# Attention followed by a maxout feed-forward layer on one core: who issues the loads of phi for batches 2 to 7

## The chip, the cores and the metric

The kernel runs on one core of one Trainium2 chip. The metric is the device time of one execution in microseconds (us), lower is better. Three runs of the kernel before the change give its time; one further execution was taken with the hardware profiler, and all durations below that are not called a median come from that one.

Engines are named as in the profile: PE is TensorE (matmuls), PEld its weight loads, DVE is VectorE, ACT is ScalarE, POOL is GpSimd, SP is SyncE, which here does nothing but issue DMAs. Sixteen DMA engines move all data. L95 is line 95 of the kernel.

## The reference

```python
a   = exp(phi - max) / sum(exp(phi - max))            # over the 576 positions; phi: 8 x 8 x 576 x 32
k_m = einsum('bhsm,bhsd->bhmd', a, k)                  # k, v, q: 8 batches x 8 heads x 576 x 64
v_m = einsum('bhsm,bhsd->bhmd', a, v)
attn = softmax(q @ k_m^T / 8)                          # 32 memory slots a head
x = (attn @ v_m) put back to rows of 512               # 4608 x 512
h = maximum(maximum(x @ w1, x @ w2), x @ w3)           # w1, w2, w3: 512 x 768
out = h @ w_out                                        # w_out: 768 x 512; out: 4608 x 512, float32
```

All inputs and the output are float32 in HBM.

## The kernel before, in words

One batch is one round of work. For batch b the kernel loads phi(b), k(b), v(b) and q(b); takes the exponential of phi (step E, ACT, L260); contracts it with k and v on PE (step B, L280); normalizes (N, DVE); turns the small result (K, or k for batches 2 to 7); transposes q on DVE (Q); makes scores on PE (S, L387) and their exponential on ACT (L396); normalizes over the slots (steps a, s, c, m and X, where m is a multiplication on POOL, L463); folds the small value matrix into the weights (D, PE, L494); and runs the feed-forward layer (F, L520 and L533; T, L567 and L582). Step T ends with a tile of 128 rows of the output in SBUF and a DMA to HBM that SP issues (L607). The first fold (D@0) needs w1; steps W, O and J before it prepare products of w3 and w_out and need those two.

Nothing of the order is left to a scheduler. A long list of tokens such as `L0@2` (step L0 of batch 2) is walked from left to right, and each engine gets its instructions in that order. Every engine's queue is in order: an instruction that waits holds back all that were issued behind it on the same engine. The token `L0@b` is `load_ph(b)`, `L1@b` and `L2@b` load k and v, `L3@b` loads q, `Y0` to `Y3` load w1, w2, w3 and w_out, and `H` loads half of k(0) or v(0).

Who issues which DMA before the change:

- SP issues phi(0), in two halves, at the very start (L93), and all output tiles but the last half one (L607, L636).
- POOL issues everything else that is loaded: k, v (L99), q (L112), phi(1) to phi(7) (L95), w1, w2, w3 (L118) and w_out (L125). k, v, q and the weights are turned from float32 to bf16 on the way; phi stays float32. Each issue takes about 0.75 us of POOL, which also runs the multiplications (L463), the repacking of k and v for batches 2 to 7 (L105) and half of the small moves (L344).

In the profile the DMAs that POOL issues are queue q0 (software_dynamic), those of SP are q1 (hardware_dynamic). The program tells of the landing of a DMA by one of eight semaphores for each of the two queues, in turn, so an issue also waits until the DMA eight places before it on its own queue has landed.

The tile for phi has two buffers (`inp`, bufs=2). phi(b) may only be loaded when the exponential of batch b-2 has read the buffer, so phi(2) waits for E@0, phi(3) for E@1, and so on. A first part of the token list shows where the loads of batch 1 and 2 stand:

```
E@0 H0@0 H2@0 L3@0 Z25@0 B0@0 ... Y2@0 G0@0 ... Y3@0 ... H1@0 H3@0 Y0@0 ... Y1@0 O1@0
L1@1 B1@0 N1@0 L0@1 O2@0! L3@1 K1@0! L2@1 ... V1@0 F0@0 F6@0 L2@2 ... L1@2 p1@0 L0@2 ...
```

`G0` makes POOL wait for the second half of k(0) before it issues more; `Z` are matmuls of zeros that keep PE busy at the start.

Of the kernel before, what the change touches and what calls it, by code (L numbers as in the profile page):

```python
# [15 lines left out]
def kernel(  # L16
# [12 lines left out]
    nc = tc.nc  # L29
# [50 lines left out]
    def by_pair(src, b):  # L80
        return src[b].rearrange("h s d -> (h s) d").rearrange(
            "(j p c) d -> p j (c d)", p=P, c=NC
        )
# [3 lines left out]
    def load_ph(b):  # L87
        ph = inp.tile([P, NP, NC, M], FP32, name="ph")
        loaded.setdefault(b, {})["ph"] = ph
        dst = ph.rearrange("p j c m -> p j (c m)")  # L90
        if b == 0:
            for h in halves:
                nc.sync.dma_start(out=dst[:, h], in_=by_pair(phi, b)[:, h])  # L93
        else:
            nc.gpsimd.dma_start(out=dst, in_=by_pair(phi, b))  # L95

# [32 lines left out]
    def wait_for(b, n):  # L129

        x = loaded[b]["q"][0:1, 0, 0, 0:2] if n else loaded[b]["kv"][0:1, 1, NP - 1, 0, 0:2]
        nc.gpsimd.tensor_copy(out=gate, in_=x)

    load_ph(0)

    warm = const.tile([P, BANK], BF16, name="warm")
# [504 lines left out]
    def issue(b, n, swap):  # L641
# [4 lines left out]
            + [nc.gpsimd.memset(x[:, :, :, 2 * D : 2 * D + 1], 1.0) for x in kvrs],  # L646
            "Y": lambda: load_w(i) if i < 3 else load_wo(),
            "L": lambda: load_ph(b) if i == 0 else load_q(b) if i == 3 else load_kv(b, i - 1),
            "H": lambda: load_kv(b, i % 2, halves[i // 2]),
            "r": lambda: pack(b, i),  # L650
# [28 lines left out]
    for w in """  # L679
# [24 lines left out]
        n, b = w.rstrip("!^").split("@")  # L704
# [31 lines left out]
```

## Time and profile before

| what | value |
|---|---|
| median of 3 runs | 163.14 us (162.96 to 163.16) |
| time of the profiled execution | 162.81 us |
| its span, first to last instruction | 161.0 us |
| granted PE clock | 1.00 throughout |
| PE busy | 152.3 us, 95% of the span |
| DVE, ACT, POOL busy | 113.9, 97.0, 81.9 us |
| phi(1) to phi(7), issued by POOL (L95) | 7 x 0.78 us, first at 13.5, last at 105.9 us |
| issue to landing of all phi loads | 3.0 to 22.5 us, median 13.4 |
| E@0 (ACT, L260) | from 3.73 to 5.15 us |

The profiled execution lies 0.33 us under the median, and 1.8 us of its time lie outside the span. In the views below a wait is put down to whatever ended it last; the chain of waits is read from the last instruction back to the first, and shows only what set the end.

### The profile page before, as it was taken

To read this page: it belongs to the slowest core of one execution; us is meant where nothing else is said; L and a number is where in the kernel's file an instruction comes from. 1 tells how busy PE (TensorE), PEld (TensorE's weight loads), DVE (VectorE), ACT (ScalarE), POOL (GpSimd) and SP (SyncE) were. 2 spreads that over 40 slices of the span, in tenths; PEclk is the share of its full clock that TensorE was granted. 3 is DMA by queue.
4 is the path that set the end of the run, shared out by engine and by line. 5 is a ranking of instruction groups with operands and counts; after the bars stand their busy time and mean duration, and the time that the engine had idled before them with its cause. 6 is when DMAs were issued, how large, how long until landed. Compare 5 with 4: busy or idle time off the path is not lost.

```text
span 161.0 us, 4938 instructions
## 1 busy us (share of the span) xinstructions
PE 152.3 (95%) x2062; PEld 84.9 (53%) x2062; DVE 113.9 (71%) x222; ACT 97.0 (60%) x179; POOL 81.9 (51%) x120
## 2 busy tenths in 40 slices
PE   7977799999999999999999999999999999999990
PEld 2432454664467446754674447656554377744460
DVE  2023456999889866877894998999898969752440
ACT  3205413934686779887997998689579884511000
POOL 7275124100699779389939989666907250000000
PEclk9999999999999999999999999999999999999999
DMA  5999999999999999999999999999712330004433
GB/s 157 147 206 208 207 209 210 242 247 210 228 312 263 275 242 269 256 259 231 269 280 258 207 310 299 218 224 284 174 69 90 116 125 0 0 0 172 158 130 132
DMA packets 21974, 31.77 MB, mean 197 GB/s; under 512 B 1216, under 2 KB 16576, under 8 KB 21952
## 3 DMA queue, kind: packets, MB, share of 16 engines
q0 software_dynamic: 16080, 21.43, 69.6%
q1 hardware_dynamic: 5728, 9.90, 17.6%
q8 instruction: 16, 0.26, 0.6%
q10 hardware_dynamic: 144, 0.13, 0.2%
q14 instruction: 6, 0.05, 0.1%
HBM read 39.32 MB, written 9.44 MB: 303 GB/s over the span
## 4 chain that ended last, share of the span: by engine, by line
PE 77%; DMA 14%; POOL 4%; DVE 2%; issue 1%; ACT 0%; POOLq 0%
PE psum L520 30%; PE psum L582 27%; DMA w_sb<-in_moe_w_dram 9%; PE psum L567 8%; PE psum L494 5%; DMA kvo<-in_k_dram 4%; PE psum L280 3%; PE psum L387 2%; POOL kvo L99 2%; PE psum L558 1%; POOL t L463 1%; DVE qT L367 1%; PE psum L618 1%; POOL wo_sb L125 0%; DVE hT L533 0%
## 5 line engine op out<-in xcount | busy, mean ns | idle before, releaser
L582 PE MATMUL psum<-wo_sb,hT 128*128 128x512 bf16 x210 | 51.3, 380 | 0.0
L520 PE MATMUL psum<-attn,wp 128*128 128x288 bf16 x384 | 50.2, 286 | 0.2 <-DVE attn L471 0.2
L520 PEld LDWEIGHTS <-wp 128*128 128x128 bf16 x384 | 37.1, 98 | 13.3 <-issue 1.3
L533 DVE TENSOR_TENSOR hT<-psum,h 128x576 bf16<-128x576 f32 x48 | 33.8, 746 | 4.9 <-PE psum L520 2.4
L582 PEld LDWEIGHTS <-hT 128*128 128x128 bf16 x210 | 19.1, 98 | 24.0 <-issue 4.8
L190 ACT CAST wp<-psum 128x1024 bf16<-128x1024 f32 (+2 forms) x33 | 26.4, 860 | 6.5 <-PE psum L494 6.5
L188 ACT ACTIVATE h<-psum 128x576 bf16<-128x576 f32 (+1 forms) x41 | 23.0, 598 | 6.4 <-PE psum L520 4.8
L105 POOL COPY kvr<-kvo 128x2304 bf16<-128x2304 bf16 x12 | 25.3, 2111 | 0.8 <-DMA kvo<-in_v_dram 0.4
L344 POOL COPY kvt<-kvm 32x96 bf16<-32x96 bf16 x48 | 12.4, 259 | 13.9 <-DVE kvm L335 6.7
L463 POOL TENSOR_TENSOR t<-t,sm 128x576 bf16<-128x576 bf16 x14 | 16.0, 1155 | 6.3 <-DVE sm L458 6.0
L567 PE MATMUL psum<-wp,attn 128*128 128x512 bf16 x62 | 18.1, 379 | 0.0
L194 DVE COPY ot<-psum 128x512 f32<-128x512 f32 x15 | 10.2, 677 | 9.9 <-PE psum L567 5.8
L190 ACT COPY ot<-psum 128x512 f32<-128x512 f32 x20 | 11.7, 592 | 8.6 <-PE psum L567 6.0
L99 POOL DMA_DIRECT2D kvo<-in_v_dram x9 | 6.6, 739 | 16.5 <-PE psum L280 13.1
L344 ACT COPY kvt<-kvm 32x96 bf16<-32x96 bf16 x48 | 12.9, 269 | 2.0 <-DVE kvm L335 1.2
L168 PE MATMUL psum<-warm 128*128 128x512 bf16 x44 | 11.8, 421 | 1.2 <-DVE warm L137 1.2
L367 DVE STREAM_TRANSPOSE qT<-qq 128x576 f32<-128x576 f32 x16 | 11.7, 749 | 1.3 <-DMA qq<-in_q_dram 1.3
L396 ACT ACTIVATE e<-psum 128x576 bf16<-128x576 f32 x16 | 9.5, 650 | 4.6 <-PE psum L387 4.5
L260 ACT ACTIVATE e<-ph 128x1152 bf16<-128x1152 f32 (+1 forms) x9 | 9.5, 1056 | 4.6 <-DMA ph<-in_phi_dram 4.4
L441 DVE STREAM_TRANSPOSE t<-e 128x288 f32<-128x288 f32 x14 | 6.6, 470 | 5.6 <-ACT e L396 5.5
L449 DVE TENSOR_REDUCE sm<-t 128x18 f32<-128x576 bf16 x14 | 10.3, 739 | 0.2
L192 DVE TENSOR_SCALAR h<-psum 128x288 bf16<-128x288 f32 (+1 forms) x17 | 9.4, 575 | 0.8 <-ACT ot L190 0.4
(62 smaller groups left out, 137.5 us busy)
## 6 DMA issues: line engine op xcount, KB each, us to landing
out_dram<-ot SPq DMA_DIRECT2D x35, 256.0 KB, 5.8
qq<-in_q_dram POOLq DMA_DIRECT2D x8, 576.0 KB, 13.5
kvo<-in_k_dram POOLq DMA_DIRECT2D x7, 576.0 KB, 16.2
ph<-in_phi_dram POOLq DMA_DIRECT2D x7, 576.0 KB, 14.3
kvo<-in_v_dram POOLq DMA_DIRECT2D x7, 576.0 KB, 17.8
w_sb<-in_moe_w_dram POOLq DMA_DIRECT2D x3, 768.0 KB, 15.1
wo_sb<-in_moe_w_out_dram POOLq DMA_DIRECT2D x1, 768.0 KB, 10.8
ph<-in_phi_dram SPq DMA_DIRECT2D x2, 288.0 KB, 3.1
```

The costliest lines, as they stand in the source:

```text
L105: nc.gpsimd.tensor_copy(out=kvrs[b % 2][:, :, :, D * i : D * (i + 1)], in_=kvos[b % 2][:, 1 - i])
L168: nc.tensor.matmul(po[:, 0:BANK], lhsT=warm[:, 0:P], rhs=warm, start=True, stop=True)
L188: nc.scalar.activation(out=out_, in_=in_, func=AF.Relu)
L190: nc.scalar.copy(out=out_, in_=in_)
L344: move(out=kvt[R * x : R * (x + 1), :, r], in_=kvm[r, x])
L367: nc.vector.transpose(out=s["qT"][:, j].rearrange("p j c r e -> p (j c r e)").bitcast(FP32), in_=loaded[b]["q"][:, j].rearrange("p j c d - ...
L449: nc.vector.tensor_reduce(out=sm, in_=s["t", g].rearrange("p n r e -> p n e r"), op=ALU.add, axis=mybir.AxisListType.X,)
L463: nc.gpsimd.tensor_tensor(out=t, in0=t, in1=s["sm", g].unsqueeze(2).to_broadcast([P, S // HP, R, 2]), op=ALU.mult,)
L520: nc.tensor.matmul(acc[:, h, 0:SH], lhsT=wps[b][:, g, w * DF + ft * P : w * DF + (ft + 1) * P], rhs=attn[:, g, c0 : c0 + SH], start=(g == ...
L533: nc.vector.tensor_tensor(out=hT[:, ft, (b % 2) * S : (b % 2 + 1) * S].rearrange("p (h n) -> p h n", h=2), in0=a, in1=s["h1", ft], op=ALU.max,
L567: nc.tensor.matmul(po, lhsT=attn[:, g, c0 : c0 + P], rhs=wp3s[b][:, g, :], start=(g == 0 and not done), stop=(last and g == NG - 1),)
L582: nc.tensor.matmul(po, lhsT=hT[:, fc, c0 : c0 + P], rhs=wo_sb[:, fc, :], start=(n == ns[0] and not done), stop=(last and n == ns[-1]),)
```

## The change

phi(2) to phi(7) are issued by SP instead of POOL, each at the place in the token list where it stood. phi(0) stays on SP in two halves, phi(1) stays on POOL.

```diff
     def load_ph(b):
         ...
         if b == 0:
             for h in halves:
                 nc.sync.dma_start(out=dst[:, h], in_=by_pair(phi, b)[:, h])
+        elif b > 1:
+            nc.sync.dma_start(out=dst, in_=by_pair(phi, b))
         else:
             nc.gpsimd.dma_start(out=dst, in_=by_pair(phi, b))
```

SP's queue after the change, in order: phi(0) in two halves, phi(2), two output tiles, phi(3), two tiles, phi(4), eight tiles, phi(5), three tiles, phi(6), three tiles, phi(7), and the remaining seventeen and a half. POOL's queue is the one before without six of its seven L95. What the two queues' instructions wait for otherwise is the same rule as before: a buffer that is free, and the DMA eight places before on the same queue. All lines behind L93 move down by two; this text uses the numbers of the kernel before.

## The prediction

> **What bounds the kernel now.** I read the page first (its busy times, its DMA row, its queues).
>
> ```profile
> PE 152.3 (95%) x2062; PEld 84.9 (53%) x2062; DVE 113.9 (71%) x222; ACT 97.0 (60%) x179; POOL 81.9 (51%) x120
> ...
> DMA  5999999999999999999999999999712330004433
> ...
> q0 software_dynamic: 16080, 21.43, 69.6%
> q1 hardware_dynamic: 5728, 9.90, 17.6%
> ```
>
> Two resources look full: PE over the whole span, and the DMA engines, whose row shows 9 from the second slice (4 us) to slice 29 (about 117 us). An average can't say which of them sets the end, so the chain of waits is next: start, length, what.
>
> ```profile
> 2.12 6.78 DMA kvo<-in_k_dram
> ...
> 9.13 0.77 POOL wo_sb L125
> ...
> 11.29 15.10 DMA w_sb<-in_moe_w_dram
> 26.39 0.14 issue
> 26.53 1.06 PE psum L494 x40
> ...
> 41.64 0.74 POOL kvo L99
> ...
> 45.25 5.79 PE psum L520 x46
> ```
>
> Until 26.39 us the chain is loads: k(0), and then w1, for which the first fold waits. From 26.53 it is PE almost without a break. The table of windows gives the two halves in numbers (columns: stretch, length, busy us of PE, PEld, DVE, ACT, POOL, clock, DMA share, GB/s written).
>
> ```profile
> 2.00:4.00 2.00, 2.00 (x6) 0.76 (x5) 0.00 (x0) 0.29 (x2) 1.93 (x5) 1.00 0.99 300
> 5.00:6.00 1.00, 1.00 (x7) 0.45 (x5) 0.00 (x0) 0.14 (x1) 0.02 (x1) 1.00 0.81 99
> 6.00:7.00 1.00, 1.00 (x6) 0.43 (x5) 0.00 (x0) 0.00 (x0) 0.00 (x0) 1.00 1.08 149
> 7.00:8.00 1.00, 1.00 (x6) 0.39 (x4) 0.00 (x0) 0.00 (x0) 0.00 (x0) 1.00 1.11 182
> ...
> 12.00:16.00 4.00, 2.93 (x42) 0.98 (x40) 1.36 (x2) 2.04 (x4) 2.33 (x4) 1.00 1.18 208
> 5.20:26.40 21.20, 17.82 (x265) 8.45 (x262) 7.32 (x14) 5.22 (x10) 8.33 (x12) 1.00 1.17 200
> 26.50:157.40 130.90, 130.49 (x1787) 74.89 (x1787) 105.64 (x201) 88.75 (x166) 69.64 (x96) 1.00 0.86 200
> ```
>
> From 26.5 to 157.4 us PE is busy 130.49 of 130.90 us: 0.41 us of idle time is all that any change behind the start can win. From 5.2 to 26.4 us the DMA engines are over 100% (packets overlap) and deliver a steady 200 GB/s of converted data: here the kernel is bound by bytes. So it is "loads until w1 is there, then 131 us of PE". A microsecond put in front of w1 is a microsecond at the end.
>
> **Where phi(2) goes.** The timeline of POOL, and then that of ACT, fix its old and new place.
>
> ```profile
> 12.78 0.79 POOL L99 DMA_DIRECT2D kvo<-in_k_dram  x1
> 13.51 0.81 POOL L95 DMA_DIRECT2D ph<-in_phi_dram  x1
> ...
> 26.94 0.75 POOL L95 DMA_DIRECT2D ph<-in_phi_dram  x1 [1.72 <-issue]
> ```
>
> ```profile
> 3.73 1.42 ACT L260 ACTIVATE e<-ph 128x576 bf16<-128x576 f32 x2 [1.71 <-DMA ph<-in_phi_dram]
> ```
>
> Before, phi(2) is the L95 at 26.94 us, behind w1, w2, k(1), phi(1), q(1), v(1), v(2) and k(2) on POOL's queue; it takes 22.5 us from issue to landing (49.4 us). After the change it is SP's third DMA, and nothing stands in front of it but phi(0). It waits only for its buffer, which E@0 gives back at 3.73 + 1.42 = 5.15 us. So it is issued at about 5.2 us, while q(0), w3 and half of k(0) are still under way and w_out, v(0) and w1 have not even been issued. The token that puts phi(2) "at its place" orders it on SP's queue alone, where the first output tile comes at 39.5 us; it does not hold it behind the loads of another queue.
>
> **Its price.** All loads that flow behind phi(2) land later by as much time of the DMA engines as phi(2) takes. Two rows bound that. On POOL's queue: k(1) and phi(1) are issued one after the other in a queue that is always full, and the view of their lines gives 20.3 and 21.1 us from issue to landing:
>
> ```profile
> DMA to landing us min/median/max: 20.3/20.3/20.3
> ```
>
> ```profile
> DMA to landing us min/median/max: 21.1/21.1/21.1
> ```
>
> k(1) lands at 12.78 + 20.3 = 33.1, phi(1) at 13.51 + 21.1 = 34.6 us, so 576 KB of phi occupy the engines for 1.5 us. On SP's queue: phi(0), the same bytes, flows nearly alone from 2 to 4 us at 300 GB/s; 0.59 MB at that rate are 1.97 us. A full price between them is likely, because the engines are shared: 1.7 us, nearer to the first row, since that is the one with the engines saturated. Below both lies what fits into room that the old queue leaves: from 5 to 8 us it delivers 99, 149 and 182 GB/s against 208 later, 0.19 MB less. If phi(2) filled all of that, a third of it would be free and the price 1.97 x 2/3 = 1.3 us; most of its data should come later, so I don't take this. The Trainium skill ("DMA: Bandwidth & Descriptors", Where 436 GB/s comes from) has a ceiling of 435 GB/s for the fabric; by it 0.59 MB would cost an estimated 1.35 us and the sum would be 164.5 us. The row is preferred, as the converted loads here read 2 x 200 = 400 GB/s at most.
>
> Could anything absorb it? PE waits for w3 at 16.0, w_out at 19.96 and w1 at 26.53 us, each right behind its landing, and then for phi(1) (E@1 starts at 34.62, on its landing) and v(1). All these loads stand behind phi(2) in time, so all shift together, and PE's work between them has no room (14.37 of 14.50 us busy from 26.5 to 41). Only behind 45 us does the missing phi(2) on POOL's queue (it took its turn before 49.4 us) give the DMA engines back what they lent; there PE is the bound and has no use for it.
>
> **The rest of the move.** POOL loses 6 issues x 0.78 = 4.7 us. POOL is on the chain from 41.64 to 44.69 us (v(3)'s issue, two multiplications L463), but phi(3)'s issue at 44.62 stands behind those, and phi(2)'s at 26.94 falls into idle time: worth 0. The cover is PE's own work; without it the gain would be at most the 0.41 us of idle time. phi(3) to phi(7) go from POOL's place to SP's: phi(3) to about 41.6 us for 44.6, phi(4) to about 51 for 52.5 (it waits for E@2, which ends at 50.7 us; the tile behind it is due at 54.6), phi(5) to 75.9 for 73.5, phi(6) to 90.1 for 88.1, phi(7) to 97.0 for 105.9. Each lands sooner than now, as SP's transfers took 6 us in the loaded stretch and POOL's 14. The loads they pass on the shared engines lose 1.5 to 2 us each time, but have gained the same from phi(2) being gone. Output tiles behind them land up to 2 us later; there are six tile buffers and at most five tiles are in flight: 0.
>
> **The sum.** On the profiled execution: span 161.0 + 1.7 = 162.7, with 1.8 outside it 164.5. Against the median, 0.33 higher: 163.14 + 1.7 = 164.8 us.
>
> **The rivals.** (1) *Slower by more.* phi(3), now on SP behind two tiles that flow at 43 to 47 us, pushes into the last of k(2), whose repacking (L105 at 48.21 us, ends at 50.33) feeds the contraction at 51.04. k(2) lands at 24.47 + 22.9 = 47.4 us, 0.8 ahead of the repacking, and the repacking may slip by 0.7. If k(2) is pushed by phi(3)'s whole 2.0 us, 0.5 us are left over and PE loses them: 165.3 us; under 1.5 us it loses nothing. Against it: most of k(2) has landed before phi(3)'s turn, and POOL is 0.81 us ahead by then, without phi(3)'s issue. (2) *No change.* The move saves only issue time and phi(2) rides in room the engines have: 163.1 us. This is what the Trainium skill's rule in "DMA: Bandwidth & Descriptors", Issuing engines are not separate DMA queues, would lead to if read as "the queue doesn't matter"; the same section also says that the queues interleave on the same 16 engines, which is the price above. For it speaks the DMA share of 0.81 at 5 us; against it the 1.17 over the whole stretch to 26.4. (3) *Faster.* POOL's chain piece at 41.64 to 45.2 us shrinks because POOL runs ahead without its L95 issues, and phi(2) costs less than that: at most -0.41, 162.7 us. It decides only if the price of phi(2) is under 0.4 us, for instance if SP's wait for the buffer ended late, behind w1; against this stand E@0's end at 5.15 us and an empty SP queue.
>
> **How the numbers follow.** Forecast (price 1.3 to 2.0 us, 164.4 to 165.2): 0.79. Rival 1: 0.12. Rival 2: 0.06. Rival 3: 0.03. A measurement of this kernel can tell about 0.2%, 0.33 us, from no change. Slower by more is then 0.91, within 0.06, faster 0.03. The range leaves out rivals 2 and 3 and reaches from a price of 1.0 (some room also behind 8 us) to rival 1 with a price of 2.2: 164.1 to 165.8 us.
>
> **What would show it.** In the profile after: SP's phi(2) issue near 5.2 us and its landing near 10 to 13 instead of 49.4; w1's landing and the first L494 near 28.2 instead of 26.5; E@1 near 36.3; PE from there as busy as before; POOL busy 77.2 us. The prediction is wrong if L494 starts at 26.5, if phi(2) is issued late, or if PE gets new gaps behind 45 us.

## The result, and the profile after

The changed kernel takes 164.98 us (median of 4 runs, 164.78 to 165.81), the kernel before 163.05 us (4 runs, 162.93 to 163.16): 1.0131 times as long, 95% interval 1.0107 to 1.0154, so 1.7 to 2.5 us slower. The profiled execution of the changed kernel is the slowest of the four, 165.81 us with a span of 164.0; the other three have spans of 163.0 to 163.2 us. What it has more than they is taken up below.

From here on lines are those of the kernel that a view is of; in the changed kernel they are two higher (the fold is L496, E is L262, the repacking L107). First the page, the same rows as before:

```profile
PE 152.4 (93%) x2062; PEld 84.8 (52%) x2062; DVE 113.9 (69%) x222; ACT 97.0 (59%) x179; POOL 77.6 (47%) x114
...
q0 software_dynamic: 15216, 17.89, 62.7%
q1 hardware_dynamic: 8896, 13.44, 24.5%
```

PE has the same 152 us of work in a longer span, POOL 4.3 us less. 3.5 MB went from q0 to q1: the move was made. SP's timeline tells when:

```profile
5.13 0.37 SPq L95 DMA_DIRECT2D ph<-in_phi_dram  x1
42.20 2.12 SPq L609 DMA_DIRECT2D out_dram<-ot  x2
44.37 0.43 SPq L95 DMA_DIRECT2D ph<-in_phi_dram  x1
```

phi(2) is issued at 5.13 us, right behind the end of E@0 (5.10 us in this execution), where POOL had issued it at 26.94. The view of that one line says how long it was under way:

```profile
DMA to landing us min/median/max: 11.0/11.0/11.0
```

It lands at 16.1 us. Its packets don't start at once: the window from 8 to 9 us counts one packet of q1, that from 9 to 10 us 82. While it flows, the DMA view of the window from 10 to 13 us counts the packets of each queue:

```profile
q0 software_dynamic: 312, 0.39, 72.6%
q1 hardware_dynamic: 313, 0.36, 41.6%
```

One packet for one packet. In a window of the kernel before without q1 (20 to 22 us) q0 moves 349 packets in 2 us, 174 a us; here it moves 104. This gives an estimate of phi(2)'s price from the trace alone: its 512 packets of data (128 partitions x 4 head pairs) take 512 / 104 = 4.9 us, in which q0 loses (174 - 104) / 174 = 40%: 2.0 us. The rule is in the Trainium skill too ("DMA: Bandwidth & Descriptors", Queues, rings and completion order): each DMA engine takes a packet from each queue in turn. The trace fits this, 312 to 313; it counts the packets and doesn't show their order.

What PE sees of it, in its timeline (start, length, what, and the idle time before it with what ended it):

```profile
28.55 0.30 PE L496 MATMUL psum<-w_sb,kvt 64*32 64x256 bf16 x8 [0.42 <-DMA w_sb<-in_moe_w_dram]
...
32.97 0.30 PE L496 MATMUL psum<-w_sb,kvt 64*32 64x256 bf16 x8 [0.32 <-DMA w_sb<-in_moe_w_dram]
...
38.59 0.80 PE L282 MATMUL psum<-kvo,e 64*32 64x128 bf16 x72 [0.22 <-ACT e L262]
```

The first fold starts at 28.55 instead of 26.53 us, 2.0 later, again right behind w1. Behind that PE runs as before; the two halves in the table of windows:

```profile
5.20:28.40 23.20, 17.75 (x264) 8.47 (x262) 7.35 (x14) 5.22 (x10) 8.34 (x12) 1.00 1.17 210
28.50:160.40 131.90, 130.66 (x1787) 74.77 (x1787) 105.62 (x201) 89.03 (x166) 65.35 (x90) 1.00 0.86 195
```

PE is busy 130.66 us behind the fold, as before (130.49), but idle 1.24 us instead of 0.41; 0.2 us of that difference is only the window, which reaches further past PE's last instruction. Most of the rest stands before 38.6 us: w2, k(1) and phi(1) land another 0.7 us late (E@1 starts at 37.37 us, 2.75 after its place before). From the first fold to the end of PE's last instruction it is 131.6 us, against 130.8 before. The profile of the kernel that moves phi(2) alone, below, has the fold at 28.29 us and 130.8 us from there, so this addition seems to belong to the one execution. It is probably most of what this execution has more than the other three, but those have no trace.

### The profile page after: what moved, and what is told of

Its sections match the earlier page's. It is cut to its first block, busy times and chain, and to the rows that moved or that the text cites. A ratio compares the mean times of both kernels' runs of the same rounds, so it can differ in the third digit from the quotient of the medians.

```text
span 164.0 us, 4935 instructions
## 1 busy us (share of the span) xinstructions
PE 152.4 (93%) x2062; PEld 84.8 (52%) x2062; DVE 113.9 (69%) x222; ACT 97.0 (59%) x179; POOL 77.6 (47%) x114
## 3 DMA queue, kind: packets, MB, share of 16 engines
q0 software_dynamic: 15216, 17.89, 62.7%
q1 hardware_dynamic: 8896, 13.44, 24.5%
## 4 chain that ended last, share of the span: by engine, by line
PE 60%; DMA 28%; POOL 6%; DVE 2%; ACT 1%; issue 1%; POOLq 0%
PE psum L522 22%; PE psum L584 22%; DMA ph<-in_phi_dram 14%; DMA kvo<-in_v_dram 10%; PE psum L569 6%; DMA kvo<-in_k_dram 4%; PE psum L496 3%; PE psum L282 3%; POOL kvo L101 2%; PE psum L389 2%; POOL t L465 1%; POOL kvr L107 1%; PE psum L560 1%; POOL w_sb L120 1%; DVE qT L369 1%
## 5 line engine op out<-in xcount | busy, mean ns | idle before, releaser
L107 POOL COPY kvr<-kvo 128x2304 bf16<-128x2304 bf16 x12 | 25.2, 2108 | 2.3 <-DMA kvo<-in_v_dram 1.4
L346 POOL COPY kvt<-kvm 32x96 bf16<-32x96 bf16 x48 | 12.5, 261 | 16.1 <-DVE kvm L337 8.8
L101 POOL DMA_DIRECT2D kvo<-in_v_dram x9 | 6.6, 739 | 20.9 <-PE psum L282 17.6
L262 ACT ACTIVATE e<-ph 128x1152 bf16<-128x1152 f32 (+1 forms) x9 | 9.5, 1056 | 4.3 <-DMA ph<-in_phi_dram 4.1
## 6 DMA issues: line engine op xcount, KB each, us to landing
kvo<-in_k_dram POOLq DMA_DIRECT2D x7, 576.0 KB, 15.7
```

Source lines behind the costliest of these rows:

```text
L107: nc.gpsimd.tensor_copy(out=kvrs[b % 2][:, :, :, D * i : D * (i + 1)], in_=kvos[b % 2][:, 1 - i])
L346: move(out=kvt[R * x : R * (x + 1), :, r], in_=kvm[r, x])
```

## The experiments

Each group of kernels was measured against the kernel before on the same chip; that one had medians of 163.0 to 163.2 us. The edits shown are cut to the lines that matter. e5, e6 and e7 are written as edits of the kernel before, the others as edits of the changed kernel.

**Where the loss is: phi(2) alone, and the rest alone.**

```diff
-        elif b > 1:
+        elif b == 2:        # e1
+        elif b > 2:         # e2
```

> Only phi(2) is issued by SP; phi(3) to phi(7) stay on POOL. My theory (phi(2) flows in front of w1 and of the loads behind it, for which PE waits one after the other): the whole loss is here, 164.8 to 165.2 us against 163.1 before; w1 lands near 28.4 us, as in the changed kernel, against 26.4. Rival A (the output tiles and phi(3) to phi(7) that share SP's queue cost the time): 163.0 to 163.3 us.

Measured: 164.66 us, ratio 1.011 (1.0076 to 1.0143). The first fold starts at 28.29 us. phi(2) alone loses 1.6 us, a little less than I expected, and can't be told from the loss of the whole change (1.0131, 1.0107 to 1.0154). Rival A, 163.0 to 163.3 us, is out as the whole cause.

> The complement: phi(3) to phi(7) on SP, phi(2) stays on POOL behind k(2). My theory: no loss, 162.8 to 163.3 us, and at most 0.4 us faster, since PE had 0.41 us of idle time behind the first fold; w1 lands at 26.4 us. Rival A: 164.5 to 165.2 us. If both this kernel and the one with phi(2) alone lose part of the 1.9 us, both theories hold in part.

Measured: 165.33 us, ratio 1.0153 (1.0123 to 1.0183). My theory had this wrong: w1 lands at 26.4 us, and yet 2.3 us are lost. Either part costs as much as both together. The trace shows another place. In POOL's timeline of the kernel before and then of this one, the repacking of v(3) (L105, L107) and the multiplications behind it:

```profile
56.57 2.11 POOL L105 COPY kvr<-kvo 128x2304 bf16<-128x2304 bf16 x1 [0.43 <-DMA kvo<-in_v_dram]
59.52 2.27 POOL L463 TENSOR_TENSOR t<-t,sm 128x576 bf16<-128x576 bf16 x2 [0.84 <-DVE sm L458]
```

```profile
59.35 2.11 POOL L107 COPY kvr<-kvo 128x2304 bf16<-128x2304 bf16 x1 [3.16 <-DMA kvo<-in_v_dram]
61.43 2.27 POOL L465 TENSOR_TENSOR t<-t,sm 128x576 bf16<-128x576 bf16 x2
```

v(3) is issued at 41.6 us in both, and is under way 14.8 us before and 17.6 us here, while phi(3) (issued at 41.67) and phi(4) (50.76) flow past it on SP's queue. POOL waits 3.16 us for it, and the multiplications for batch 2, which stand behind the repacking in POOL's queue, come 1.9 us later. PE waits for their result: the view lists no wait of PE between 55 and 70 us before, and here

```profile
PE psum L522 <- DVE attn L473: 1.6, 2, 0.9
```

So a load that overtakes others costs wherever one of those is due. Four kernels take this apart.

```diff
+        elif b == 3:            # e8
+        elif b in (3, 4):       # e9
+        elif b > 3:             # e10
+        elif b in (3, 5, 6, 7): # e12
```

> phi(3) alone on SP. With phi(3) to phi(7) on SP and phi(2) on POOL the kernel lost 2.3 us, which I had not expected; in that trace v(3) lands 2.8 us later, its repacking on POOL waits 3.2 us for it, and the multiplications that PE waits for stand behind the repacking. New theory (D): any phi that passes v(3) costs there what goes over a slack of some 0.8 us. phi(3) alone passes with its 1.6 to 2.0 us: v(3) lands near 58.2 us instead of 56.4, and the time is 163.8 to 164.4 us. Rival E (the loss comes from phi(4), sent at 50.8 us, or from the later ones): 163.0 to 163.3 us.

> phi(3) and phi(4) on SP, the rest on POOL. phi(3) alone lost 0.1 us (163.1), which missed my 163.8 to 164.4; phi(3) to phi(7) lost 2.3 us. If theory D still holds with both in front of v(3) (phi(3) uses up the slack, phi(4) adds its bytes), v(3) lands near 59 us and nearly the whole loss of phi(3) to phi(7) is here: 164.4 to 165.3 us. If the loss comes from phi(5) to phi(7) (theory F), 163.0 to 163.4 us.

> The complement: phi(4) to phi(7) on SP, phi(2) and phi(3) on POOL. Theory D: phi(4) passes at most a part of v(3) and phi(3) still stands behind it, so v(3) is up to 1 us late and the loss small, 163.0 to 163.6 us. Theory F: 164.5 to 165.3 us.

> Only the loads that should overtake nothing that is due: phi(3), phi(5), phi(6) and phi(7) on SP, phi(2) and phi(4) on POOL. phi(3) alone lost 0.1 us, phi(4) to phi(7) lost 0.7 us. By theory D (only what passes w1 and its followers, or v(3) beyond its slack, costs) the whole 0.7 us was phi(4)'s: 162.9 to 163.4 us here, with four of seven loads moved. If phi(5) to phi(7) cost time of their own, 163.6 to 164.2 us.

| on SP's queue | v(3) under way in the profile, us | median, us | ratio (95% interval) |
|---|---|---|---|
| none (before) | 14.8 | 163.0 | |
| phi(3) (e8) | 16.4 | 163.08 | 1.001 (0.9991 to 1.0028) |
| phi(3), (5), (6), (7) (e12) | 16.3 | 163.49 | 1.0019 (0.9993 to 1.0046) |
| phi(4) to phi(7) (e10) | 15.7 | 163.78 | 1.0038 (1.0014 to 1.0062) |
| phi(3) to phi(7) (e2) | 17.6 | 165.33 | 1.0153 (1.0123 to 1.0183) |
| phi(3), phi(4) (e9) | 18.0 | 165.79 | 1.0152 (1.0116 to 1.0187) |

phi(3) alone was expected to cost 0.8 us or more and costs nothing that can be measured, though its profile shows v(3) 1.6 us longer under way and PE waiting 0.6 us for what stands behind it. With phi(4) behind it the whole loss of e2 is there, and without phi(4) (e12) it is gone within the interval. e10 costs 0.1% to 0.6%; its median is 0.2 us over the range that I expected. In its profile PE doesn't wait behind v(3) at all, but behind the repacking of the next load, k(3), which phi(4) passes too. POOL's timeline and PE's waits:

```profile
65.39 2.10 POOL L107 COPY kvr<-kvo 128x2304 bf16<-128x2304 bf16 x1 [2.69 <-DMA kvo<-in_k_dram]
```

```profile
PE psum L282 <- POOL kvr L107: 0.9, 1, 0.9
```

So the loss of e2 needs phi(3) and phi(4) together, and the waits in its trace stand behind v(3). That it is so much more than the sum of the two (e8 and e10) fits a slack at v(3) that the first uses up, but this is argued from profiles, one of each kernel: no run holds phi(4) back until v(3) has landed, and how large the slack is in an average run isn't settled.

Why doesn't the changed kernel lose 4 us, then? With phi(2) gone from POOL's queue, v(3) no longer stands behind its 576 KB. The profiles bear this out: with phi(2) alone moved (e1) v(3) is under way 13.6 us, before 14.8, in the changed kernel 15.9, and with phi(2) left on POOL (e2) 17.6. What phi(2) costs at the start it pays back in part there; what phi(3) and phi(4) take, they take from that. In the profile after, PE's waits between 55 and 70 us are under the view's threshold, but nothing is left over. The chain of waits that set the end now runs through v(3), where before it was PE's own work:

```profile
44.34 15.88 DMA kvo<-in_v_dram
...
60.34 2.11 POOL kvr L107
62.45 2.25 POOL t L465 x2
```

**How much is in front: doses.** Half of phi(2) early, all of it twice, and all of it early on POOL's queue.

```diff
+        elif b == 2:                                                     # e6
+            nc.sync.dma_start(out=dst[:, halves[0]], in_=by_pair(phi, b)[:, halves[0]])
+            nc.gpsimd.dma_start(out=dst[:, halves[1]], in_=by_pair(phi, b)[:, halves[1]])
...
+            for _ in range(2 if b == 2 else 1):                          # e7
+                nc.sync.dma_start(out=dst, in_=by_pair(phi, b))
...
-        ... Y2@0 G0@0 ... p1@0 L0@2 F3@0 ...                             # e5, in the kernel before
+        ... Y2@0 L0@2 G0@0 ... p1@0 F3@0 ...
```

> A smaller dose: the first half of phi(2) goes early on SP, the second half stays on POOL at its old place; phi(3) to phi(7) on POOL. phi(2) alone on SP cost 1.6 us. By my theory (bytes in front) half of that, 0.7 to 1.0 us: 163.7 to 164.1 us, w1 at about 27.3 us. If the cost is one of the issue or of a wait, whatever the size (rival C): 164.6 us again.

Measured: 163.51 us, ratio 1.0031 (1.0008 to 1.0054), first fold at 27.09 us, 0.56 later than before. The loss is 0.5 us, a third of e1's and under the range that I expected. The fold alone proves little here: in eight profiles in which phi(2) isn't sent before 25 us (the kernel before, e2, e3, e4, e8, e9, e10, e12) it starts anywhere from 25.85 to 27.40 us. Why half the bytes cost less than half isn't settled.

> A larger dose: the changed kernel, with phi(2) loaded twice into its tile, the second time when the first has landed (near 16 us), still in front of w1. By my theory w1 comes 4 us later than before, near 30.4 us, and the time is 166.6 to 167.2 us. If room in the DMA queues were filled (the rival of no change), or a fixed cost were paid once: 165 us.

Measured: 166.49 us, ratio 1.0233 (1.0195 to 1.0272), first fold at 29.93 us, 3.4 later. A second dose costs the changed kernel another 1.5 us. A cost paid once, or room in the queues that takes in all of phi(2), is ruled out; room for a part of it, as the small cost of the half (e6) would allow, is not.

> SP isn't used for phi(2) at all: the kernel before, with phi(2)'s load moved forward in POOL's own queue, right behind w3's (near 5 us). phi(3) to phi(7) stay on POOL at their places. If it is the place in the order of bytes that costs (my theory), w_out, v(0) and w1 land about 1.5 us later (phi(1) took 1.5 us of this queue), w3 as before, and the time is 164.4 to 164.9 us. If it is SP's queue or the hardware's way of issuing (rival B), no loss: 163.0 to 163.3 us.

Measured: 165.32 us, ratio 1.0135 (1.0096 to 1.0174). No load but phi(0) is on SP's queue, and the loss is as large as in the changed kernel. It is the place among the bytes, not the issuing engine. That it is larger than the expected 1.4 to 1.9 us may have a cause that I hadn't thought of. In the profile, k(0) lands 1.25 us later than in that of before, and w_out with it; PE's timeline and the windows of this kernel:

```profile
22.24 4.44 PE L227 MATMUL psum<-wo_sb,w3T 128*128 128x512 bf16 x12 [2.63 <-DMA wo_sb<-in_moe_w_out_dram]
```

```profile
22.55:25.96 3.41, 3.41 (x10) 1.21 (x8) 1.24 (x2) 0.00 (x0) 0.57 (x1) 0.50 1.16 210
```

After an idle gap of 2.63 us PE runs for 3.41 us at a granted clock of 0.50, and twelve matmuls that take 2.75 us in the other traces take 4.44. The Trainium skill ("TensorE: Matmul & The Clock Gate", What's actually happening) describes this: a free-running window of 3413 ns decides on half or full clock. The length agrees. Half the runs of e5 have a mean clock of 0.99 (one such stretch takes 0.01 off the mean): 166.53, 165.73 and 165.42 us, against 164.33, 165.21 and 164.67 of the others. The median of the others is inside the expected range.

**Can the loss be held off?** The same six loads on SP, with phi(2) made to wait.

```diff
             if b == 2:
+                nc.gpsimd.memset(ph[0:1, 0, 0, 0:1], 0.0)                         # e3
+                nc.gpsimd.tensor_copy(out=ph[0:1, 0, 0, 0:2],                     # e4, L0@2 behind L3@2
+                                      in_=kvos[1][0:1, 0, NP - 1, 0, 0:2])
             nc.sync.dma_start(out=dst, in_=by_pair(phi, b))
```

> As the changed kernel, but phi(2) isn't sent at 5.2 us: POOL writes one element of phi's tile at the old place of the load, near 25 us, and SP's load of that tile waits for it. w1 is then as before (26.4 us), but phi(2) goes in front of the rest of w2, k(1), phi(1) and q(1), which are still in POOL's queue. My theory in its wide form (each of these loads is waited for, up to v(1) at 40 us): nearly the full loss again, 164.3 to 165.1 us, with the first fold at 26.5 us but the exponential E@1 1.5 to 2 us later than before. Narrow form (only w1 counts, PE has work in hand behind it): 163.0 to 163.3 us. Rival A: 165 us, with E@1 as before.

Measured: 165.38 us, ratio 1.0151 (1.012 to 1.0181). The wide form of the theory holds, with a loss 0.3 us over the range. PE's timeline:

```profile
26.91 0.30 PE L498 MATMUL psum<-w_sb,kvt 64*32 64x256 bf16 x8 [0.36 <-DMA w_sb<-in_moe_w_dram]
...
38.21 0.80 PE L284 MATMUL psum<-kvo,e 64*32 64x128 bf16 x72 [1.72 <-ACT e L264]
```

w1 is nearly in time, and PE then waits 1.72 us for E@1, whose phi(1) phi(2) has overtaken. Protecting w1 alone moves the gap ten us further and closes none of it.

> As the changed kernel, but phi(2) is held until v(1) has landed (40.1 us): POOL copies two elements of v(1) into phi's tile while it has nothing else to do, and SP's load waits for that. Nothing that PE waits for before 41 us then stands behind phi(2). My theory: the loss is gone, 162.9 to 163.4 us, although all six loads are on SP's queue. Rival A: still 164.5 to 165 us. If phi(2) now lands too late for E@2 (due near 49 us), some tenths are lost there, with ACT waiting for phi.

Measured: 163.75 us, ratio 1.0049 (1.0024 to 1.0075). Two thirds of the loss are gone with all six loads on SP's queue; SP's queue as such isn't the main cause. What is left, 0.4 to 1.2 us, is over my range. The profile has ACT waiting 0.96 us for phi(2) before E@2, as feared, and phi(1) landing late in that execution; which of the two the median has isn't settled.

**The clock.**

```diff
-        ... Z9@0 S@0 ... W2@0 H1@0 H3@0 Y0@0 Z6@0 O0@0! ...
+        ... Z14@0 S@0 ... W2@0 H1@0 H3@0 Y0@0 Z10@0 O0@0! ...
```

> The changed kernel with nine more of the zero matmuls at the start: five ahead of the scores of batch 0, four ahead of the first product of w3 and w_out. Two profiles of kernels with an early phi(2) show one stretch of 3.41 us at half of PE's clock near 16 and 23 us, behind idle gaps of PE, and about 4 in 10 runs of these kernels have a mean clock of 0.99 or less, against 2 in 39 of the kernel before. If such stretches carry part of the loss, they vanish with the gaps filled, and the median falls by some 0.3 us to 164.4 to 164.8; the rest of the loss (w1 2 us late) stays. If the clock plays no part: 164.8 to 165.2 us as the changed kernel.

Measured: 165.87 us, ratio 1.0166 (1.0129 to 1.0203): slower, against both expectations, and with a mean clock of 0.99 in three of four runs. The added matmuls end before w3 lands, PE then idles 1.54 us, and the half-clock stretch begins there; the window from 17.85 us:

```profile
17.85:21.20 3.35, 3.34 (x26) 2.84 (x27) 1.87 (x3) 0.69 (x2) 0.74 (x1) 0.50 1.23 207
```

The added zero matmuls in front of the first product then run in part at half speed and hold it back: it starts at 22.97 us, 1.4 behind the landing of w_out. So this says nothing on the share of the clock in the changed kernel. Its own runs say a little: the one with a mean clock of 0.99 took 164.96 us, those with 0.996 or more 164.78 to 165.81. There the clock isn't visible in the time.

## Why the prediction was right

1.7 us were forecast, 1.93 measured (difference of the medians), inside the range of 164.1 to 165.8 us. By its steps:

- **"Loads until w1 is there, then 131 us of PE"** held. The fold moved by 2.0 us (1.8 in e1), and PE's busy time behind it by 0.2.
- **Where phi(2) goes**: issued at 5.13 us for 5.2. Held, and tested: the loss comes also from POOL's queue (e5), and most of it goes when phi(2) waits (e4).
- **Its price**, 1.7 us, was chosen between 1.5 (POOL's queue) and 1.97 (SP's queue alone). The packets give an estimate of 2.0, the first folds 1.8 (e1) and 2.0, the medians 1.6 (e1) and 1.9; with folds that scatter by 1.5 us from profile to profile these can't be told from 1.7. The reason for the choice was wrong all the same. I took the first row as the nearer because the engines were saturated there, but on POOL's queue phi is sent in larger packets: by the profile's page the six loads left q0 with 864 packets less (16080 to 15216, 144 for each load) and gave q1 3168 more (5728 to 8896, 528 for each). What counts, if the queues share by packets, is the number of packets that SP's queue makes of it. That 1.7 came so near is partly luck. The ceiling that the prediction took from the Trainium skill ("DMA: Bandwidth & Descriptors", Where 436 GB/s comes from), by which the price would be an estimated 1.35 us, was further off.
- **The landing** at 10 to 13 us was wrong: it was 16.1. The 6 us that I read for SP's transfers are those of output tiles of 256 KB; phi's 576 KB took 11.0 us, with nearly 4 us gone before the first packets.
- **All loads behind it shift together** held, and e3 shows that it isn't w1 alone: with w1 nearly in time the loss is as large.
- **"The rest of the move: 0"** held for the change as a whole and would have been wrong for the part. The sentence that the loads overtaken "have gained the same from phi(2) being gone" carried the weight: e2 takes that gain away, and phi(3) and phi(4) cost 2.3 to 2.8 us (e2, e9). My expectation for e2 forgot it. The prediction didn't look at v(3), where the two effects meet with nothing to spare, so that they came out even is luck in part.
- **Rivals.** The first had the right kind of event at the wrong load: not k(2) but v(3) is due. In the changed kernel neither costs much. The second and third are out by the loss itself and by the doses: it grows with the bytes in front.
- POOL's 77.6 us busy (77.2 forecast) bought nothing: PE, not POOL, sets the end there.

## What to carry to other kernels

A place in a token list or a program orders a load only on its own queue. On another queue it is issued as soon as its buffer is free, and once its packets flow (here nearly 4 us later) it takes about every second one from the other queue. So ask what is due while it flows, not only when it is issued. A kernel whose loads stand in one queue in the order of need has that order as its schedule: take one out and both the ones it passes and the ones it no longer delays move.

## What the runs showed of the hardware that I had not expected

- Two queues that both have work share the DMA engines by packets, not by bytes: 312 to 313 in 3 us beside phi(2), and in the profile after, from 54 to 55 us beside output data, 90 to 91 packets with 0.10 to 0.18 MB.
- A 576 KB load on SP's queue takes 11.0 us from issue to landing beside a full q0, where a half of phi(0), 288 KB, took 3.0 us near the start.
- PE fell to half its clock for 3.41 us after idle gaps of 1.54 us (e11) and 2.63 us (e5), both shorter than the stretch itself. In e6 it did so from 16.1 us on behind no gap over 0.66 us, and in e7 it kept its full clock after a gap of 2.00 us: the length of one gap doesn't tell.
